# Sliding-window attention and a SwiGLU block: AV and scores in one block of 64x64 PE tiles per chunk

## Chip, cores, metric

One NeuronCore of a Trainium2 chip (trn2). The metric is the device time of one execution in microseconds (us).

A ratio of two kernels is the mean time of the one's fast runs over the mean time of the other's fast runs of the same rounds, on the same chip, with a 95% interval. It is not quite the ratio of the medians, which are quoted beside it.

## The reference, cut

Causal attention with a window of 64 keys, then a gated feed-forward block:

```python
# q, k, v: (8, 8, 576, 64) float32; w_gate, w_val: (512, 1536); w_out: (1536, 512)
scores = (q @ k.T) / 8                       # per batch and head
mask = (rel >= 0) & (rel < 64)               # rel = query position - key position
attn = softmax(where(mask, scores, -1e9))
x = (attn @ v), heads joined                 # (4608, 512)
g = x @ w_gate
out = ((g * sigmoid(g)) * (x @ w_val)) @ w_out
```

## The kernel before

The 4608 tokens are worked in 36 *chunks* of 128; four chunks are a *group* of 512 (groups 0 to 8). Every operation is recorded in a graph, which adds the semaphores; the order on an engine is the order in which operations are recorded. The engines are named as in the profile: PE is TensorE (matmuls), PEld its weight loads, ACT ScalarE, DVE VectorE, POOL GpSimd, SP SyncE. Matmuls write into eight PSUM banks, ps, of 128 x 512 float32, which the kernel hands out in rings. PE's array can be used whole or in smaller tiles; the size of the tiles is the *tiling mode*, and 64*128 in a line of the profile is a tile of 64 rows and 128 columns. The names used below:

- **S(n)**, scores of chunk n: PE matmuls, exp on ACT (two, one per half of the heads), two multiplications by a 0/1 mask on VectorE.
- **A(n)** or AV: probabilities times V on PE; then on VectorE a reciprocal and a division (L467 and L470 before the change) for each half. The division writes xb.
- **XD(n)**: DMA transpose of xb into xT, the input of the feed-forward. Groups 0 and 1 transpose on PE instead (**X(n)**).
- **F(c, f)**: for group c and feature block f, four matmuls into a G bank and four into a V bank; tanh (sig) on ACT; uu and hT on VectorE. Twelve per group.
- **O(c, u)**: twelve matmuls for 128 output rows, a copy on ACT, a store.

A query sees its own 64-key block and the one before. The kernel before forms, for each 64 queries, a matmul over 128 consecutive keys. For that it needs V twice: va, and vb, which is va shifted by 64 keys and made by DMA copies.

```python
    # S: per 64 queries (w) a window of 128 keys; one 64x128 PE tile per head
    for w in range(2):
        k0 = 128 * n + 64 * w
        for c in range(4):
            for h in range(2):
                ps = slice(64 * h, 64 * h + 64)
                r = e.matmul(sv[h][:, w, c], self.kT[ps, c, k0:k0 + 128],
                             qT[ps, c, 64 * w:64 * w + 64], ...)
    # AV: contraction over 128 keys; 64 queries of output per 128x64 PE tile
    for j in range(4):
        h = 2 * j + half
        for w, vv in ((0, vb), (1, va)):
            r = e.matmul(av[64*w:64*w+64, j, :], pt[:, h, 64*w:64*w+64], vv[:, h, 0:65],
                         start=True, stop=True)
    # [...] PSUM banks: F rotates over four, O has one of its own, the rest over three
    self.rot = {"f": ([0, 1, 2, 3], 0), "o": ([4], 0), "a": ([5, 6, 7], 0)}
    # [...] steady loop, groups 2 to 7; n = 4c+u+4
    self.F(c, 3 * u)
    self.A(n)
    self.TD(n + 3)             # DMA transposes of K and Q, three chunks ahead
    self.F(c, 3 * u + 1)
    self.S(n + 1)
    self.XD(n)
    self.copy_v(n + 3)
    self.O(c - 1, u)
    self.F(c, 3 * u + 2)
```

The softmax here doesn't subtract the row's maximum and nothing guards it: scores larger than these inputs give would overflow.

## Time and profile before

| | before |
|---|---|
| median of 3 runs | 350.76 us (350.25 to 352.24) |
| span of the profiled run | 349.7 us |
| PE busy | 94% |
| period of one chunk, groups 4 to 6 | 8.70 us |
| of it three F, one O, attention | 5.19, 2.60, 0.91 us |

The page's first part, busy time and share of the span; from the groups, AV on PE (columns: line, engine, operation, tiles, count, busy us, mean ns, idle before it):

```profile
PE 328.2 (94%) x2615; PEld 159.2 (46%) x2659; DVE 216.1 (62%) x461; ACT 140.9 (40%) x248; POOL 108.5 (31%) x141
...
L461 PE MATMUL ps<-va,pt 128*64 128x65 bf16 x288 | 15.6, 198 | 0.0
L461 PE MATMUL ps<-vb,pt 128*64 128x65 bf16 x288 | 15.6, 198 | 0.1
```

A busy share does not tell what one chunk pays. The timeline does (columns: start us, duration us, engine, line, operation; in brackets idle time before it and what ended it). PE, one chunk, the sixteen AV rows between 194.55 and 194.79 cut to the first:

```profile
193.59 1.03 PE L515 MATMUL ps<-xT,Wv 128*128 128x512 bf16 x3
194.55 0.22 PE L461 MATMUL ps<-vb,pt 128*64 128x65 bf16 x1
...
194.92 1.04 PE L515 MATMUL ps<-xT,Wg 128*128 128x512 bf16 x4
195.79 1.03 PE L515 MATMUL ps<-xT,Wv 128*128 128x512 bf16 x4
196.75 0.41 PE L432 MATMUL ps<-qT,kT 64*128 64x64 bf16 x16
197.09 2.76 PE L539 MATMUL ps<-Wo,hT 128*128 128x512 bf16 x11
```

Matmuls of 512 columns start 0.216 us apart, so four need 0.86 us, but their row lasts 1.03 us: a duration includes about 0.17 us of pipeline latency, and the cost of a row is read from start to start. Four V matmuls from 193.59 end streaming at 194.45; the next F starts at 194.92: AV costs 0.47 us. Scores cost 0.44 us (196.65 to 197.09). (One of the V matmuls is missing from the record.) No idle is left between these rows: PE is the bound.

VectorE in the same chunk:

```profile
195.75 0.17 DVE L467 RECIPROCAL rc<-ps 128x4 f32<-128x4 f32 x1
195.96 0.42 DVE L470 TENSOR_TENSOR xb<-ps,rc 128x256 bf16<-128x256 f32 x1
...
196.50 0.42 DVE L470 TENSOR_TENSOR xb<-ps,rc 128x256 bf16<-128x256 f32 x1
...
198.16 0.75 DVE L448 TENSOR_TENSOR pt<-pt,mask 128x512 bf16<-128x512 bf16 x2
```

The divisions follow AV at once and the masks come last, where there is time.

The last thing to see is a group boundary: the first F of a group needs xT of all four chunks. PE, start of group 4:

```profile
166.63 1.04 PE L515 MATMUL ps<-xT,Wg 128*128 128x512 bf16 x4 [0.30 <-DMA xT<-xb]
```

The transpose of the fourth chunk arrives 0.30 us late here, and 0.18 us late at group 3; at the later boundaries it is in time. (These idle times are the brackets of the timeline. They count from the recorded end of the matmul before, so each is short by the 0.17 us of latency; all boundary idle is given so.)

### The profile page before, as it was taken

The page shows a single profiled execution, that of the slowest core. Times are in us where ns is not written, and L with a number is a line of the kernel's source. Part 1 is how long each engine was busy: PE and PEld are TensorE (multiplying, and loading weights), DVE is VectorE, ACT ScalarE, POOL GpSimd, SP SyncE. Part 2 cuts the span into 40 slices and gives each one's busy share as a digit, 9 for nine tenths or more (in the row PEclk, how much of TensorE's full clock was granted, in tenths as well). Part 3 has the DMA queues.
Part 4 walks back from the last instruction along what each step waited for, and adds up shares of the span by engine and source line. Part 5 has one row for each costly group of instructions (what it writes and reads, how often), then busy time and mean ns, then how long its engine had stood idle before and what let it go on. Part 6 is the DMA issues. An engine that isn't in the chain of part 4 may idle for free.

```text
span 349.7 us, 6706 instructions
## 1 busy us (share of the span) xinstructions
PE 328.2 (94%) x2615; PEld 159.2 (46%) x2659; DVE 216.1 (62%) x461; ACT 140.9 (40%) x248; POOL 108.5 (31%) x141
## 2 busy tenths in 40 slices
PE   6686997899999999999999999999999999999996
PEld 2454443554444444444444444444444444444444
DVE  4655583478966666666666666666666666655520
ACT  3652444555543333444344444444433333232321
POOL 8996523364633343323232243222000000000000
PEclk9899899999999999999999999999999999999999
DMA  8999999999999999999999999999833311100012
GB/s 205 189 213 175 214 161 202 146 154 142 166 97 144 148 135 142 138 138 146 132 138 140 142 116 164 125 162 128 138 97 97 88 49 47 64 32 30 30 46 106
DMA packets 167279, 44.82 MB, mean 128 GB/s; under 512 B 147408, under 2 KB 162768, under 8 KB 167248
## 3 DMA queue, kind: packets, MB, share of 16 engines
q0 software_dynamic: 113152, 17.83, 71.7%
q1 hardware_dynamic: 51872, 25.38, 33.1%
q10 hardware_dynamic: 2224, 1.18, 1.3%
q8 instruction: 21, 0.34, 0.4%
q14 instruction: 10, 0.08, 0.1%
HBM read 37.75 MB, written 9.44 MB: 135 GB/s over the span
## 4 chain that ended last, share of the span: by engine, by line
PE 73%; DVE 10%; DMA 7%; POOL 5%; ACT 3%; issue 1%; POOLq 0%
PE ps L515 42%; PE ps L539 25%; DMA kn<-in_k_dram 4%; DVE uu L523 4%; DMA xT<-xb 3%; DVE hT L525 3%; PE ps L432 3%; PE ps L461 2%; ACT sig L521 2%; POOL Wg L365 2%; POOL Wv L365 1%; DVE xb L470 1%; PE ps L568 1%; POOL va L343 1%; PE ps L383 1%
## 5 line engine op out<-in xcount | busy, mean ns | idle before, releaser
L523 DVE SCALAR_TENSOR_TENSOR uu<-sig,ps 128x512 bf16<-128x512 bf16 (+1 forms) x112 | 74.4, 665 | 92.6 <-ACT sig L521 92.5
L515 PE MATMUL ps<-xT,Wg 128*128 128x512 bf16 (+1 forms) x435 | 110.2, 374 | 2.6 <-DVE uu L523 1.0
L515 PE MATMUL ps<-xT,Wv 128*128 128x512 bf16 (+1 forms) x433 | 111.3, 373 | 0.8
L521 ACT ACTIVATE sig<-ps 128x512 bf16<-128x512 f32 (+1 forms) x112 | 65.2, 582 | 95.0 <-PE ps L515 95.0
L539 PE MATMUL ps<-Wo,hT 128*128 128x512 bf16 x404 | 94.1, 379 | 3.8 <-DVE hT L525 1.7
L525 DVE SCALAR_TENSOR_TENSOR hT<-uu,ps 128x512 bf16<-128x512 bf16 (+1 forms) x112 | 74.8, 668 | 4.3 <-PE ps L515 0.5
L515 PEld LDWEIGHTS ps<-xT,Wv 128*128 128x128 bf16 x448 | 44.0, 98 | 50.1 <-issue 1.1
L343 POOL DMA_DIRECT2D va<-in_v_dram x40 | 34.1, 856 | 98.8 <-PE ps L461 97.5
L539 PEld LDWEIGHTS ps<-Wo,hT 128*128 128x128 bf16 x420 | 38.8, 98 | 46.1 <-DVE hT L525 1.6
L515 PEld LDWEIGHTS ps<-xT,Wg 128*128 128x128 bf16 x448 | 40.3, 98 | 42.8 <-DMA xT<-xb 1.5
L443 ACT ACTIVATE pt<-ps 128x512 bf16<-128x512 f32 x72 | 39.0, 596 | 21.5 <-PE ps L432 21.5
L551 ACT ACTIVATE ost<-ps 128x512 f32<-128x512 f32 x35 | 20.9, 597 | 62.3 <-PE ps L539 62.3
L267 POOL DMA_DIRECT2D qn<-in_q_dram x36 | 30.3, 844 | 38.6 <-PE ps L383 24.4
L470 DVE TENSOR_TENSOR xb<-ps,rc 128x256 bf16<-128x256 f32 x72 | 30.5, 424 | 2.5
L267 POOL DMA_DIRECT2D kn<-in_k_dram x36 | 30.5, 852 | 1.6 <-DMA qn<-in_q_dram 0.8
L448 DVE TENSOR_TENSOR pt<-pt,mask 128x512 bf16<-128x512 bf16 x64 | 24.4, 419 | 3.7 <-ACT pt L443 3.5
L461 PEld LDWEIGHTS ps<-vb,pt 128*64 128x64 bf16 x288 | 11.7, 110 | 13.4 <-DVE hT L525 9.7
L432 PEld LDWEIGHTS ps<-qT,kT 64*128 64x128 bf16 x576 | 10.4, 95 | 16.2 <-DVE rc L467 10.6
L432 PE MATMUL ps<-qT,kT 64*128 64x64 bf16 x576 | 14.5, 191 | 1.8 <-DVE xb L470 1.6
L461 PE MATMUL ps<-va,pt 128*64 128x65 bf16 x288 | 15.6, 198 | 0.0
L461 PE MATMUL ps<-vb,pt 128*64 128x65 bf16 x288 | 15.6, 198 | 0.1
L467 DVE RECIPROCAL rc<-ps 128x4 f32<-128x4 f32 x72 | 12.4, 172 | 0.9 <-PE ps L461 0.9
(52 smaller groups left out, 96.6 us busy)
## 6 DMA issues: line engine op xcount, KB each, us to landing
out_dram<-ost SPq DMA_DIRECT2D x35, 256.0 KB, 2.9
vb<-va SPq DMA_DIRECT2D x68, 80.0 KB, 4.1
va<-in_v_dram POOLq DMA_DIRECT2D x32, 128.0 KB, 4.7
qn<-in_q_dram POOLq DMA_DIRECT2D x28, 128.0 KB, 4.9
kn<-in_k_dram POOLq DMA_DIRECT2D x28, 128.0 KB, 5.3
Wo<-in_moe_w_out_dram POOLq DMA_DIRECT2D x2, 768.0 KB, 18.5
Wg<-in_moe_w_gate_dram POOLq DMA_DIRECT2D x5, 256.0 KB, 13.1
Wv<-in_moe_w_val_dram POOLq DMA_DIRECT2D x5, 256.0 KB, 13.6
```

What stands on the lines that cost most here:

```text
L267: self.g.op("pool", lambda e, d=d, a=a: e.dma_start(d, a), writes=ks, dma=True)
L343: g.op("pool", lambda e, d=d, a=a: e.dma_start(d, a), writes=ks, dma=True)
L432: r = e.matmul(sv[h][:, w, c], self.kT[ps, c, k0:k0 + 128], qT[ps, c, 64 * w:64 * w + 64], start=not biased, stop=not biased or (w == 1 an ...
L443: g.op("act", lambda e, po=po, si=si: e.activation(po, si, ACTF.Exp, scale=SCALE), reads=[bk], writes=[pk])
L448: g.op("dve", lambda e, po=po, m=m: e.tensor_tensor(po, po, m, ALU.mult), reads=[pk, "mask"], writes=[pk])
L461: r = e.matmul(av[64 * w:64 * w + 64, j, :], pt[:, h, 64 * w:64 * w + 64], vv[:, h, 0:65], start=True, stop=True)
L470: g.op("dve", lambda e: e.tensor_tensor(xo, av[:, :, 0:64], rb, ALU.mult), reads=[bk, ("rc", ir)], writes=[("xb", ix, half)])
L515: r = e.matmul(bank[:, 0:n], W[:, kk, f * 128:f * 128 + 128], xT[:, kk, t0:t1], start=(kk == 0), stop=(kk == NK - 1))
L521: g.op("act", lambda e: e.activation(sig[:, 0:n], G[:, 0:n], ACTF.Tanh, scale=0.5), reads=[gk], writes=[("sig", i)])
L523: g.op("dve", lambda e: e.scalar_tensor_tensor(uu[:, 0:n], sig[:, 0:n], 1.0, G[:, 0:n], ALU.add, ALU.mult), reads=[("sig", i), gk], writes ...
L525: g.op("dve", lambda e: e.scalar_tensor_tensor(hT[:, f, t0:t1], uu[:, 0:n], 0.5, V[:, 0:n], ALU.mult, ALU.mult), reads=[("uu", i), vk], wr ...
L539: r = e.matmul(OB[:, :], hT[:, f, 128 * u:128 * u + 128], self.Wo[:, f, :], start=(f == 0), stop=(f == NF - 1))
```

## The change

Intent: contract over aligned blocks of 64 keys, so that both scores and AV use 64x64 tiles, four at a time, in the same tiling mode. Then the scores of the next chunk can stand inside AV of this one, with fewer changes of tiling mode; V is needed once, without shifted copies; and one mask serves all chunks. AV of one head and 64 queries becomes two accumulating matmuls on two row tiles. To keep two row tiles from writing one PSUM bank at the same time (the rule is in the last section), AV has two phases, and the second waits for the end of the first; the scores fill this wait.

```diff
-        self.rot = {"f": ([0, 1, 2, 3], 0), "o": ([4], 0), "a": ([5, 6, 7], 0)}
+        self.rot = {"f": ([0, 1, 2, 3], 0), "a": ([4, 5, 6, 7], 0)}
 [...] S
-                for c in range(4):
+            for c in range(4):
+                for o, q0, q1, kk in ((0, 0, 128, k0), (64, 0, 64, k0 - 64), (64, 64, 128, k0 + 64)):
                     for h in range(2):
-                        r = e.matmul(sv[h][:, w, c], self.kT[ps, c, k0:k0 + 128],
-                                     qT[ps, c, 64 * w:64 * w + 64], ...)
+                        r = e.matmul(sv[h][o:o + 64, c, q0:q1], self.kT[ps, c, kk:kk + 64], qT[ps, c, q0:q1], ...)
 [...] A(n, mid): 16 matmuls of phase 0, then mid(), then 16 of phase 1
+        first = g.op("pe", phase(0), reads=rd, writes=wr)
+        if mid is not None:
+            mid()
+        g.op("pe", phase(1), reads=rd, writes=wr, after=[first])
         [...] then, for each half, reciprocal and division on VectorE
 [...] steady loop
                 self.F(c, 3 * u)
-                if live:
-                    self.A(n)
+                if live:
+                    self.A(n, (lambda: self.S(n + 1)) if n + 1 < NCH else None)
 [...]          self.TD(n + 3)
+                if live and c > 1:
+                    self.XD(n)
                 self.F(c, 3 * u + 1)
-                [...] self.S(n + 1); self.XD(n); self.copy_v(n + 3)
                 self.O(c - 1, u)            # its bank now comes from "a", no longer from "o"
                 self.F(c, 3 * u + 2)
```

`mid()` records all of S, its VectorE masks too, ahead of the divisions of A. Groups 0 and 1 and the start are rearranged in the same manner; there O takes banks of the F ring.

More of the change, by code (lines that the diff above doesn't have):

```diff
@@ L40, in __init__, with op @@
         self.readers = {}
-    def op(self, eng, fn, reads=(), writes=(), dma=False):
-        deps = {}
+    def op(self, eng, fn, reads=(), writes=(), dma=False, after=()):
+        deps = {o.i: (o, "sync") for o in after}
         for k in reads:
             for w in self.writers.get(k, ()):
-                deps[w.i] = (w, "raw")
+                deps.setdefault(w.i, (w, "raw"))
         for k in writes:
@@ L86, in emit @@
             for d, kind in deps:
-                if d.eng == e and not d.dma and (e == "pe" or kind != "raw") and not o.dma and e != "pool":
+                if kind != "sync" and d.eng == e and not d.dma and (e == "pe" or kind != "raw") and not o.dma and e != "pool":
                     continue
@@ L176, in alloc @@
         self.ident = sb("ident", 128)
-        self.mask = sb("mask", 4 * 64)
+        self.mask = sb("mask", 128)
         self.Wg = sb("Wg", NK * DFF)[:, :].rearrange("p (c f) -> p c f", c=NK)
@@ L184, in alloc @@
         self.va = [hd(t) for t in ring("va", self.NV, H * 80)]
-        self.vb = [hd(t) for t in ring("vb", self.NV, H * 80)]
         self.kT = sb("kT", 4 * (T + 64))[:, :].rearrange("p (c t) -> p c t", c=4)
@@ L191, in alloc @@
         self.cq, self.ck = [[t.rearrange("p (j h d) -> p j h d", j=2, h=H) for t in st(x, BF)] for x in ("cq", "ck")]
-        self.nmask = sb("nmask", 4 * 64)
+        self.nmask = sb("nmask", 128)
         self.wz = sb("wz", 512)
@@ L233, in init @@
         g.op("dve", lambda e: e.memset(self.kT[:, :, 0:64], 0.0), writes=[("kT", -1, p) for p in range(4)])
-        g.op("dve", lambda e: e.memset(self.vb[0][0:64, :, 0:66], 0.0), writes=[("vb", 0, 0)])
         self.init_va(0)
@@ L240, in init_va @@
             va = self.va[i]
-            g.op(eng, lambda e, va=va: e.memset(va[:, :, 64:80], 1.0), writes=[("va", i)])
+            g.op(eng, lambda e, va=va: e.memset(va[:, :, 64:80], 1.0), writes=[("va", i)],
+                 after=[self.last_sel] if eng == "pool" else [])
     def init_pool_a(self):
@@ L249, in init_mask @@
     def init_mask(self, m, key, fill):
-        mm = m[:, :].rearrange("p (a q) -> p a q", a=4)
-        self.g.op("pool", lambda e: e.affine_select(
-            out=mm, in_=mm, compare_op=ALU.is_gt, fill=fill, base=0,
-            pattern=[[0, 4], [-1, 64]], channel_multiplier=1), writes=[key])
-        self.g.op("pool", lambda e: e.affine_select(
-            out=mm, in_=mm, compare_op=ALU.is_ge, fill=fill, base=64,
-            pattern=[[0, 4], [1, 64]], channel_multiplier=-1), writes=[key])
-        self.g.op("pool", lambda e: e.memset(m[0:64, 128:192], fill), writes=[key])
+        for p0, c0, op in ((0, 0, ALU.is_ge), (0, 64, ALU.is_gt), (64, 0, ALU.is_gt), (64, 64, ALU.is_ge)):
+            d = m[p0:p0 + 64, c0:c0 + 64]
+            sg = 1 if op == ALU.is_gt else -1
+            self.last_sel = self.g.op("pool", lambda e, d=d, op=op, sg=sg: e.affine_select(
+                out=d, in_=d, compare_op=op, fill=fill, base=0,
+                pattern=[[-sg, 64]], channel_multiplier=sg), writes=[key])
     def load_qk(self, n):
@@ L284, in first_cast @@
             self.g.op("act", lambda e: e.activation(d, a, ACTF.Copy), reads=rk, writes=wk)
-    def first_vb(self, n, part, eng):
-        i = n + 1 - part
-        dst = self.vb[i][64:128] if part else self.vb[i][0:64]
-        src = self.va[n][0:64] if part else self.va[n][64:128]
-        rd, wr = [("va", n, 0), ("va", n, 1), ("va", n)], [("vb", i, part)]
-        if eng == "dve":
-            self.g.op("dve", lambda e: e.tensor_copy(dst, src), reads=rd, writes=wr)
-        else:
-            self.g.op("sp", lambda e: e.dma_start(dst, src), reads=rd, writes=wr, dma=True)
     def first_T(self, which, st):
@@ L332, in warm, with load_v @@
         self.g.op("pe", pe, reads=["wz"], writes=[bk])
-    def load_v(self, n, copy=True):
+    def load_v(self, n):
         g = self.g
@@ L343, in load_v @@
             g.op("pool", lambda e, d=d, a=a: e.dma_start(d, a), writes=ks, dma=True)
-        if copy:
-            self.copy_v(n)
-    def copy_v(self, n):
-        g = self.g
-        i = n % self.NV
-        va = self.va[i]
-        parts = list(self.segs(128 * n, 128))
-        vb = self.vb[i]
-        lo = [("va", i, 0), ("va", i)]
-        hi = [("va", i, 0 if len(parts) == 1 else 1), ("va", i)]
-        g.op("sp", lambda e: e.dma_start(vb[64:128], va[0:64]), reads=lo, writes=[("vb", i, 1)], dma=True)
-        if n + 1 < NCH:
-            i2 = (n + 1) % self.NV
-            vb2 = self.vb[i2]
-            g.op("sp", lambda e: e.dma_start(vb2[0:64], va[64:128]), reads=hi, writes=[("vb", i2, 0)], dma=True)
     def load_w(self, which, a, b):
@@ L401, in TD @@
              writes=[("qT", iz, p) for p in range(4)], dma=True)
-    def variant(self, n):
-        b0 = (2 * n) % BPB == 0
-        b1 = (2 * n + 1) % BPB == 0
-        return slice(2, 4) if b0 else (slice(1, 3) if b1 else slice(0, 2))
     def bias(self, n):
         bb = [self.bank("a") for _ in range(2)]
-        nm = self.nmask[:, :].rearrange("p (a q) -> p a q", a=4)[:, self.variant(n)].unsqueeze(2).to_broadcast([128, 2, 4, 64])
+        nm = self.nmask[:, :].unsqueeze(1).to_broadcast([128, 4, 128])
         for bank, bk in bb:
-            bv = bank[:, :].rearrange("p (w c q) -> p w c q", w=2, c=4)
+            bv = bank[:, :].rearrange("p (c q) -> p c q", c=4)
             self.g.op("pe", lambda e, bv=bv: e.matmul(bv, self.ident[:, :], nm, start=True, stop=False),
@@ L423, in S @@
             bb = [self.bank("a") for _ in range(2)]
-        sv = [b[:, :].rearrange("p (w c q) -> p w c q", w=2, c=4) for b, _ in bb]
+        sv = [b[:, :].rearrange("p (c q) -> p c q", c=4) for b, _ in bb]
+        k0 = 128 * n + 64
         def pe(e):
-            for w in range(2):
-                k0 = 128 * n + 64 * w
-                for c in range(4):
+            for c in range(4):
+                for o, q0, q1, kk in ((0, 0, 128, k0), (64, 0, 64, k0 - 64), (64, 64, 128, k0 + 64)):
                     for h in range(2):
                         ps = slice(64 * h, 64 * h + 64)
-                        r = e.matmul(sv[h][:, w, c], self.kT[ps, c, k0:k0 + 128],
-                                     qT[ps, c, 64 * w:64 * w + 64], start=not biased,
-                                     stop=not biased or (w == 1 and c == 3))
+                        r = e.matmul(sv[h][o:o + 64, c, q0:q1], self.kT[ps, c, kk:kk + 64], qT[ps, c, q0:q1],
+                                     start=not biased, stop=not biased or c == 3 and kk != k0 - 64)
             return r
@@ L439, in S @@
         for h, (bank, bk) in enumerate(bb):
-            po = pt.rearrange("p (c e) (w q) -> p e w c q", e=2, w=2)[:, h]
-            si = bank[:, :].rearrange("p (w c q) -> p w c q", w=2, c=4)
+            po = pt.rearrange("p (c e) q -> p e c q", e=2)[:, h]
+            si = bank[:, :].rearrange("p (c q) -> p c q", c=4)
             pk = ("pt", ip, h)
@@ L445, in S, with A @@
                 continue
-            m = self.mask[:, :].rearrange("p (a q) -> p a q", a=4)[:, self.variant(n)]
-            m = m.unsqueeze(2).to_broadcast([128, 2, 4, 64])
+            m = self.mask[:, :].unsqueeze(1).to_broadcast([128, 4, 128])
             g.op("dve", lambda e, po=po, m=m: e.tensor_tensor(po, po, m, ALU.mult), reads=[pk, "mask"], writes=[pk])
-    def AV(self, n, half):
+    def A(self, n, mid=None):
         g = self.g
-        iv, ip, ix = n % self.NV, n % self.NP, n % 4
-        va, vb, pt = self.va[iv], self.vb[iv], self.pt[ip]
-        bank, bk = self.bank("a")
-        av = bank[:, 0:260].rearrange("p (h x) -> p h x", h=4)
-        def pe(e):
-            for j in range(4):
-                h = 2 * j + half
-                for w, vv in ((0, vb), (1, va)):
-                    r = e.matmul(av[64 * w:64 * w + 64, j, :], pt[:, h, 64 * w:64 * w + 64], vv[:, h, 0:65], start=True, stop=True)
-            return r
-        g.op("pe", pe, reads=[("pt", ip, half), ("va", iv), ("va", iv, 0), ("va", iv, 1), ("vb", iv, 0), ("vb", iv, 1)], writes=[bk])
-        ir = (2 * n + half) % 4
-        rc = self.rc[ir]
-        g.op("dve", lambda e: e.reciprocal(rc[:, :].unsqueeze(2), av[:, :, 64:65]), reads=[bk], writes=[("rc", ir)])
-        xo = self.xb[ix][:, :].rearrange("p (c e d) -> p e c d", e=2, d=64)[:, half]
-        rb = rc[:, :].unsqueeze(2).to_broadcast([128, 4, 64])
-        g.op("dve", lambda e: e.tensor_tensor(xo, av[:, :, 0:64], rb, ALU.mult),
-             reads=[bk, ("rc", ir)], writes=[("xb", ix, half)])
@@ new lines, in A @@
+        ip, ix = n % self.NP, n % 4
+        va, vp, pt = self.va[n % self.NV], self.va[(n - 1) % self.NV], self.pt[ip]
+        bb = [self.bank("a") for _ in range(2)]
+        av = [b[:, 0:260].rearrange("p (h x) -> p h x", h=4) for b, _ in bb]
+        seq = {}
+        for step in range(2):
+            for j in range(4):
+                for half in range(2):
+                    kp = half ^ step
+                    for w in range(2):
+                        if kp == w or (2 * n + w) % BPB:
+                            seq.setdefault((half, w), []).append((step, j, kp))
@@ new lines, in phase, with pe @@
+        def phase(step):
+            def pe(e):
+                for j in range(4):
+                    for w in range(2):
+                        for half in range(2):
+                            q = seq[half, w]
+                            key = (step, j, half ^ step)
+                            if key not in q:
+                                continue
+                            kp, h = half ^ step, 4 * half + j
+                            vv = vp if kp > w else va
+                            ks = slice(64 * kp, 64 * kp + 64)
+                            ws = slice(64 * w, 64 * w + 64)
+                            r = e.matmul(av[half][ws, j, :], pt[ks, h, ws], vv[ks, h, 0:65],
+                                         start=key == q[0], stop=key == q[-1])
+                return r
+            return pe
@@ new lines, in A @@
+        vk = [("va", m % self.NV, j) for m in ((n - 1, n) if n else (n,)) for j in range(2)]
+        vk += [("va", m % self.NV) for m in ((n - 1, n) if n else (n,))]
+        rd = [("pt", ip, 0), ("pt", ip, 1)] + vk
+        wr = [bk for _, bk in bb]
+        first = g.op("pe", phase(0), reads=rd, writes=wr)
+        if mid is not None:
+            mid()
+        g.op("pe", phase(1), reads=rd, writes=wr, after=[first])
+        for half, (bank, bk) in enumerate(bb):
+            ir = (2 * n + half) % 4
+            rc = self.rc[ir]
+            g.op("dve", lambda e, rc=rc, a=av[half]: e.reciprocal(rc[:, :].unsqueeze(2), a[:, :, 64:65]), reads=[bk], writes=[("rc", ir)])
+            xo = self.xb[ix][:, 256 * half:256 * half + 256].rearrange("p (h d) -> p h d", h=4)
+            rb = rc[:, :].unsqueeze(2).to_broadcast([128, 4, 64])
+            g.op("dve", lambda e, xo=xo, rb=rb, a=av[half]: e.tensor_tensor(xo, a[:, :, 0:64], rb, ALU.mult),
+                 reads=[bk, ("rc", ir)], writes=[("xb", ix, half)])
@@ L526, in F, with O @@
              reads=[("uu", i), vk], writes=[("hT", ih, f)])
-    def O(self, c, u, mid=None):
+    def O(self, c, u, mid=None, kind="a"):
         g = self.g
@@ L533, in O @@
         ost = self.ost[io]
-        OB, ok = self.bank("o")
+        OB, ok = self.bank(kind)
         def part(f0, f1):
@@ L562, in O_last @@
         for w, eng in ((0, "act"), (1, "dve")):
-            OB, ok = self.bank("o")
+            OB, ok = self.bank("a")
             cs = slice(256 * w, 256 * w + 256)
@@ L579, in O_last, with load @@
             g.op(q, lambda e, d=d, cs=cs: e.dma_start(self.out[r0:r0 + 128, cs], d), reads=[("osth", w)], dma=True)
-    def A(self, n):
-        self.AV(n, 0)
-        self.AV(n, 1)
     def build(self):
         W = lambda a, b: (self.load_w("g", a, b), self.load_w("v", a, b))
-        def load(n, copy=True):
+        def load(n):
             if n < NCH:
                 self.load_qk(n)
-                self.load_v(n, copy)
+                self.load_v(n)
         self.first_loads()
         self.init()
-        self.load_v(0, False)
+        self.load_v(0)
         self.init_pool_a()
-        self.load_v(1, False)
+        self.load_v(1)
         self.init_mask(self.nmask, "nmask", -30000.0)
@@ L600, in build @@
         W(1, 2)
-        self.load_v(2, False)
-        self.load_v(3, False)
+        self.load_v(2)
+        self.load_v(3)
         for f in range(2, 12, 2):
@@ L619, in build @@
         self.S(1, b1)
-        self.first_vb(0, 1, "dve")
         self.first_cast("k", 1)
@@ L623, in build @@
         tk = self.first_T("k", 1)
-        self.first_vb(0, 0, "dve")
-        self.first_vb(1, 1, "dve")
-        for n, part in ((1, 0), (2, 1), (2, 0), (3, 1), (3, 0)):
-            self.first_vb(n, part, "sp")
         self.A(0)
@@ L637, in build @@
         self.banks("a", [5, 6, 7, 4])
-        b2, b3 = self.bias(2), self.bias(3)
+        b2 = self.bias(2)
         self.F(0, 0, 0, 256)
+        b3 = self.bias(3)
         self.S(2, b2)
+        self.S(3, b3)
         self.F(0, 1, 0, 256)
-        self.S(3, b3)
+        self.F(0, 2, 0, 256)
         self.A(2)
-        self.F(0, 2, 0, 256)
         self.A(3)
+        self.F(0, 3, 0, 256)
         self.X(2, "act")
-        self.F(0, 3, 0, 256)
         self.X(3, "act")
-        self.banks("a", [5, 6, 7])
         self.init_va(4, "pool")
@@ L665, in build @@
         self.F(0, 7)
-        self.A(4)
+        self.A(4, lambda: self.S(5))
         self.F(0, 8)
-        self.S(5)
         load(7)
@@ L671, in build @@
         self.X(4, "act")
-        self.A(5)
+        self.T(6)
         self.F(0, 10)
-        self.T(6)
+        self.A(5, lambda: self.S(6))
         self.F(0, 11)
         self.X(5, "act")
+        self.T(7)
         load(8)
-        self.S(6)
-        self.O(0, 0)
-        self.T(7)
+        self.O(0, 0, None, "f")
+        self.A(6, lambda: self.S(7))
         load(9)
-        self.A(6)
-        self.O(0, 1)
-        self.S(7)
-        def mid():
-            self.X(6, "act")
-            self.T(8)
-        self.O(0, 2, mid)
-        self.A(7)
-        self.S(8)
-        self.O(0, 3, lambda: self.X(7, "act"))
+        self.O(0, 1, None, "f")
+        self.X(6, "act")
+        self.T(8)
+        self.O(0, 2, None, "f")
+        self.A(7, lambda: self.S(8))
+        self.O(0, 3, lambda: self.X(7, "act"), "f")
         self.T(9)
         load(10)
-        load(11, False)
+        load(11)
         for c in range(1, NFC):
@@ L700, in build @@
                 live = n < NCH
-                load(n + 4, False)
-                last = u == 3
-                late = c == NFC - 1 and last
+                load(n + 4)
+                late = c == NFC - 1 and u == 3
                 self.F(c, 3 * u)
                 if live:
-                    self.A(n)
+                    self.A(n, (lambda: self.S(n + 1)) if n + 1 < NCH else None)
                 if n + 3 < NCH and n + 3 >= self.ND:
                     self.TD(n + 3)
+                if live and c > 1:
+                    self.XD(n)
                 self.F(c, 3 * u + 1)
-                if live:
-                    if n + 1 < NCH:
-                        self.S(n + 1)
-                    if c > 1:
-                        self.XD(n)
-                    elif last:
-                        self.X(n, "act")
-                    if n + 3 < NCH:
-                        self.copy_v(n + 3)
                 if c > 1 and not late:
                     self.O(c - 1, u)
+                if live and c == 1 and u == 3:
+                    self.X(n, "act")
                 self.F(c, 3 * u + 2)
-                if live and c == 1 and not last:
+                if live and c == 1 and u < 3:
                     self.X(n, "act")
@@ L727, in build @@
                     self.O(c - 1, u)
-        self.banks("o", [0, 1, 2, 3])
         for u in range(3):
```

## The prediction

> **What bounds the kernel now.** TensorE. The page gives PE 94% busy; the chain of waits is 73% PE. From 190 us on, the timeline repeats one period per 128-token chunk, 8.69 us, with no PE idle in it: three F (8 matmuls, 1.73 us each), one O (12, 2.60 us), and 0.91 us of attention. AV costs 0.47 us (stream end of F 194.45, next F 194.92), scores 0.44 us (196.65 to 197.09). Only about 0.25 us of each is streaming (AV pairs start every 31 ns, score pairs every 27 ns); the rest is about 0.10 us on entering and 0.10 us on leaving. The Trainium skill, "TensorEngine Tiling (Array Packing)", Key Properties, says a change of tiling mode drains the engine; the gaps agree.
>
> **What the change saves.** With four 64x64 tiles AV still runs 8 matmuls per tile, so I expect no shorter stream; scores likewise (512 columns per tile). One block instead of two saves two of four mode changes, 0.20 us; the wait of the second AV phase on the first, beside scores of 0.24 us and a matmul latency of 0.20 us, gives back about 0.06. Block: about 0.77 us, saving 0.14 us per chunk, some 4 us in all if nothing else moved. The 68 V copies (5.4 MB of 44.8) go. At the start PE waits 2.65 us for K of chunk 4 (31.5 to 34.2), queued behind weights and five V copies; I expect it 1 to 2 us earlier. Chunks 4 to 11 save about 1 us more.
>
> **What it adds on the critical path.** VectorE and the banks. A and scores take four banks, O the fifth of a ring of four, so O gets AV half 0's bank and must wait for its division. That division is now queued behind both score masks. From the end of the first F (t=0): scores start 0.23, both exps end 0.45+1.08 later (as at 65.63 to 67.16), masks free VectorE at 2.15, reciprocal 0.21, division 0.42, 0.06 to PE: O starts at 2.85 to 2.95. Before, O starts at 2.64. So the period becomes about 8.95 us: +0.26 us over 24 chunks (groups 2 to 7), +6 us, although the PE block is shorter; PE will sit idle about 0.4 us before each O.
>
> Second, the last division ends at 3.3 instead of 2.5, so the DMA transpose xT<-xb of a group's fourth chunk starts 0.9 us later, with only 3.9 us until the next group's first F. It took 4.8 us at groups 2 and 3 (stall 0.3 us then), 2.3 to 3.3 later. V buffers are now held one chunk longer, so the V, Q, K loads run together just before it. I expect stalls near 1 us at two to four boundaries: +2 to +3 us.
>
> **Sum.** 350.8 - 2.5 (start and groups 0, 1) + 6 + 2.5 = 357; I shade towards no change: 355.5 us, 8 in 10 between 348.5 and 361. Faster by over 2%: 0.04; within 2%: 0.63; slower by over 2%: 0.33.
>
> **What would show it.** Right: PE idle before O released by the division xb; period 8.9 to 9.0 us; block near 0.77 us; xT<-xb ending idle at group boundaries; K of chunk 4 landing before 33 us. Wrong: no idle before O and period near 8.5; or a block over 1 us, meaning that 64x64 matmuls issue slower than four per 30 ns.
>
> **What would make it wrong.** Slower issue of 56 small matmuls (slower); two-fold faster AV streams, V copies holding up DMA more than I think, or a larger gain at the start, where the cold clock after the wait costs 1.6 us (faster).

## The result

| | before | after |
|---|---|---|
| median | 351.19 us (4 runs, 350.25 to 352.24) | 361.10 us (4 runs, 360.19 to 361.61) |
| ratio | | 1.0278 (1.024 to 1.0317) |
| span of the profiled run | 349.7 us | 359.2 us |
| first F of group 1 | 69.24 us | 66.91 us |
| first F of group 2 | 96.25 us | 94.53 us |
| first F of group 4 | 166.63 us | 169.32 us |
| first F of group 6 | 236.21 us | 243.67 us |

The change is slower by 2.8%. The last four rows, read from the PE timelines, show where: until group 2 the kernel after is 1.7 us ahead, and it loses from there on. The page's first part after:

```profile
PE 331.8 (92%) x3459; PEld 158.4 (44%) x3459; DVE 218.3 (61%) x457; ACT 140.9 (39%) x248; POOL 108.9 (30%) x143
...
L442 PE MATMUL ps<-va,pt 64*64 64x65 bf16 x1088 | 22.7, 197 | 0.4
```

PE, one chunk, after:

```profile
197.00 1.03 PE L506 MATMUL ps<-xT,Wv 128*128 128x512 bf16 x4
197.96 0.32 PE L442 MATMUL ps<-va,pt 64*64 64x65 bf16 x16
198.10 0.42 PE L398 MATMUL ps<-qT,kT 64*64 64x128 bf16 x24
198.35 0.32 PE L442 MATMUL ps<-va,pt 64*64 64x65 bf16 x16
198.60 1.04 PE L506 MATMUL ps<-xT,Wg 128*128 128x512 bf16 x4
199.48 1.03 PE L506 MATMUL ps<-xT,Wv 128*128 128x512 bf16 x4
200.72 2.76 PE L530 MATMUL ps<-Wo,hT 128*128 128x512 bf16 x12 [0.22 <-DVE xb L461]
```

The block itself is a success. The F before it ends streaming at 197.86 and the F after it starts at 198.60: 0.74 us, against 0.91 us for the two parts before. But O starts at 200.72, while the F before it ends streaming at 199.48 + 0.86 = 200.34. PE loses 0.38 us there. (The bracket says 0.22 us; it is short by the latency.) VectorE says why:

```profile
199.20 0.91 DVE L412 TENSOR_TENSOR pt<-pt,mask 128x512 bf16<-128x512 bf16 x2
200.03 0.17 DVE L458 RECIPROCAL rc<-ps 128x4 f32<-128x4 f32 x1
200.24 0.42 DVE L461 TENSOR_TENSOR xb<-ps,rc 128x256 bf16<-128x256 f32 x1
...
200.79 0.42 DVE L461 TENSOR_TENSOR xb<-ps,rc 128x256 bf16<-128x256 f32 x1
```

The masks now come first. Half 0's division ends at 200.66, and O, whose bank is that of AV half 0, starts 0.06 us later. The last division ends at 201.21, 3.35 us after the first F; before, at 196.92, it was 2.47 us.

The list of waits after the change names the same wait (columns: who waited for whom, us in total, times, longest):

```profile
PE ps L530 <- DVE xb L461: 5.8, 23, 0.3
...
PE ps L506 <- DVE hT L516: 3.0, 2, 1.6
PE ps L506 <- DVE uu L514: 2.3, 2, 1.2
```

The other two rows are the group boundaries, four idle times of 1.59, 1.20, 1.43 and 1.13 us, 5.35 us in all against 0.48 us before. Group 5 begins so, PE, the DMA queue (SP) and POOL, which issues the loads of V, Q and K:

```profile
204.19 1.03 PE L506 MATMUL ps<-xT,Wv 128*128 128x512 bf16 x4
206.64 1.02 PE L506 MATMUL ps<-xT,Wg 128*128 128x512 bf16 x4 [1.43 <-DVE hT L516]
```

```profile
201.24 1.21 SPq L488 DMA_TRANSPOSE xT<-xb  x1
```

```profile
199.97 0.88 POOL L264 DMA_DIRECT2D qn<-in_q_dram  x1
200.84 0.90 POOL L264 DMA_DIRECT2D kn<-in_k_dram  x1
```

PE's wait is put down to VectorE's hT, which belongs to the previous F, whose banks this F does not use. The DMA transpose issued at 201.24 landed 5.3 us later, at 206.5; the F starts 0.1 us after that. So the transpose is the likely releaser, and an experiment below tests it. At this boundary the kernel before saw a landing of 2.6 us and no wait; there the Q load was issued after the transpose, and not 1.3 us before it. SP and POOL before, then the landing of this transpose after and before (from the view of tile xT):

```profile
196.95 1.19 SPq L497 DMA_TRANSPOSE xT<-xb  x1
197.57 0.88 POOL L267 DMA_DIRECT2D qn<-in_q_dram  x1 [1.30 <-DMA qT<-qn]
```

```profile
DMA to landing us min/median/max: 5.3/5.3/5.3
```

```profile
DMA to landing us min/median/max: 2.6/2.6/2.6
```

The span grew by 9.5 us: -1.7 us until group 2, +4.9 us of boundary idle (5.35 - 0.48), and a remainder of 6.3 us over 24 chunks, 0.26 us each. The timeline confirms the remainder: group 6, at whose end no boundary waits, takes 35.83 us (243.67 to 279.50), 8.96 us per chunk against 8.70. It is the wait before O, 0.42 us on average (5.8 us in 23 brackets, and 0.17 us more each), less the 0.17 us that the block saves.

### The profile page after: what moved, and what is told of

It reads as the page before. It is cut to its first block, busy times and chain, and to the rows that moved or that the text cites. A ratio compares the mean times of both kernels' runs of the same rounds, so it can differ in the third digit from the quotient of the medians.

```text
span 359.2 us, 8166 instructions
## 1 busy us (share of the span) xinstructions
PE 331.8 (92%) x3459; PEld 158.4 (44%) x3459; DVE 218.3 (61%) x457; ACT 140.9 (39%) x248; POOL 108.9 (30%) x143
## 4 chain that ended last, share of the span: by engine, by line
PE 62%; DVE 14%; ACT 10%; DMA 7%; POOL 3%; issue 3%; SPq 0%
PE ps L506 30%; PE ps L530 26%; ACT pt L408 8%; DMA kn<-in_k_dram 5%; DVE xb L461 4%; DVE pt L412 4%; DVE uu L514 3%; DMA fk<-in_k_dram 3%; PE ps L442 2%; PE ps L398 2%; DVE hT L516 2%; DVE rc L458 1%; ACT sig L512 1%; POOL qn L264 1%; PE ps L559 1%
## 5 line engine op out<-in xcount | busy, mean ns | idle before, releaser
L506 PE MATMUL ps<-xT,Wg 128*128 128x512 bf16 (+1 forms) x448 | 111.9, 372 | 6.3 <-DVE hT L516 3.0
L530 PE MATMUL ps<-Wo,hT 128*128 128x512 bf16 x420 | 96.3, 380 | 6.3 <-DVE xb L461 5.8
L412 DVE TENSOR_TENSOR pt<-pt,mask 128x512 bf16<-128x512 bf16 x64 | 26.8, 425 | 8.9 <-ACT pt L408 7.0
L442 PE MATMUL ps<-va,pt 64*64 64x65 bf16 x1088 | 22.7, 197 | 0.4
L442 PEld LDWEIGHTS ps<-va,pt 64*64 64x64 bf16 x1088 | 15.0, 106 | 14.8 <-issue 12.7
L398 PE MATMUL ps<-qT,kT 64*64 64x64 bf16 (+1 forms) x864 | 15.5, 201 | 0.6 <-ACT qT L360 0.5
L398 PEld LDWEIGHTS ps<-qT,kT 64*64 64x64 bf16 x864 | 12.3, 108 | 2.1 <-ACT qT L360 0.8
L482 ACT ACTIVATE xT<-ps 128x512 bf16<-128x512 bf16 x12 | 7.2, 596 | 8.6 <-PE ps L473 8.6
```

The lines of the kernel that those rows point to most:

```text
L398: r = e.matmul(sv[h][o:o + 64, c, q0:q1], self.kT[ps, c, kk:kk + 64], qT[ps, c, q0:q1], start=not biased, stop=not biased or c == 3 and kk ...
L412: g.op("dve", lambda e, po=po, m=m: e.tensor_tensor(po, po, m, ALU.mult), reads=[pk, "mask"], writes=[pk])
L442: r = e.matmul(av[half][ws, j, :], pt[ks, h, ws], vv[ks, h, 0:65], start=key == q[0], stop=key == q[-1])
L506: r = e.matmul(bank[:, 0:n], W[:, kk, f * 128:f * 128 + 128], xT[:, kk, t0:t1], start=(kk == 0), stop=(kk == NK - 1))
L530: r = e.matmul(OB[:, :], hT[:, f, 128 * u:128 * u + 128], self.Wo[:, f, :], start=(f == 0), stop=(f == NF - 1))
```

## The experiments

My theory after the result: the new tiles and the block are good, and all the loss comes from one late event, the divisions, through two consumers, the bank that O takes and the fourth chunk's transpose. The first rival is that the 64x64 block itself costs more than it saves. The second is that the boundary waits are what the profile says, VectorE's uu and hT. Each ratio is against the kernel before, in the same rounds on the same chip. Differences to the kernel after are between rounds: the median of the kernel before was 351.19 us in its round and 350.12, 350.71 and 351.65 us in those of the experiments, so a difference of about 1 us between medians of different rounds is not resolved; for small terms the traces decide.

| run | median us | ratio (95%) |
|---|---|---|
| after | 361.10 | 1.0278 (1.024 to 1.0317) |
| e1_o_f | 352.81 | 1.0084 (1.0047 to 1.0121) |
| e2_div_first | 347.03 | 0.9906 (0.9883 to 0.9929) |
| e3_nv7 | 358.62 | 1.0249 (1.0215 to 1.0282) |
| e4_x_act | 355.90 | 1.0176 (1.014 to 1.0212) |
| e5_split | 359.36 | 1.024 (1.0198 to 1.0282) |
| e7_div_nv7 | 346.35 | 0.9869 (0.983 to 0.9908) |
| e8_copies | 364.51 | 1.0401 (1.0362 to 1.044) |
| e9_div_x | 344.30 | 0.9817 (0.978 to 0.9853) |
| e10_of_x | 346.21 | 0.9854 (0.982 to 0.9888) |
| e6_div_nv7_x | 344.26 | 0.98 (0.976 to 0.9839) |

All ten gave a correct result. All edits are to the kernel after the change.

### O in another bank (e1_o_f)

```diff
-                    self.O(c - 1, u)
+                    self.O(c - 1, u, None, "f" if live else "a")
```

> O of groups 2 to 7 takes a bank of the F ring, so it no longer shares one with AV half 0; nothing else moves. Bank theory (O waits for the division because of the shared bank): PE idle before O ended by the division xb goes from 5.8 us in all to near 0, the chunk period from 8.9-9.0 to about 8.6 us, but the transpose xT<-xb starts as late as before against an earlier next group, so each boundary stall grows by about 0.3 us: total about 361 - 6 + 1.2 = 356 us. Rival (the 64x64 block itself is what got dearer): O starts no earlier and the time stays at 361.

Measured: 352.81 us. (The trace is of the slowest of its four runs, 354.84 us; the reason is given with e8.) PE at the same place, start of group 5:

```profile
197.58 1.03 PE L506 MATMUL ps<-xT,Wv 128*128 128x512 bf16 x4
198.44 2.75 PE L530 MATMUL ps<-Wo,hT 128*128 128x512 bf16 x12
...
201.90 1.03 PE L506 MATMUL ps<-xT,Wv 128*128 128x512 bf16 x4
204.77 1.02 PE L506 MATMUL ps<-xT,Wg 128*128 128x512 bf16 x4 [1.84 <-DVE hT L516]
```

O follows F without a gap, and the period is 8.52 us (groups 6 and 7, where no boundary waits: 34.08 us for four chunks). The boundary idle was 1.49, 1.79, 1.84 and 1.59 us, 6.7 us in all instead of 5.35: of what O gave back, a third of a microsecond per boundary, on average, was lost at the next wait, as expected. The gain was larger than I had written, 8.3 us instead of 5: I had counted the change of the period (0.26 us) and not the wait (0.38 us). The shared bank is shown to be one of the two causes, and the first rival falls: with the same block of 64x64 matmuls the period is 0.18 us shorter than before the change.

### Divisions ahead of the masks (e2_div_first)

```diff
 in S:
-            g.op("dve", ... mask multiplication ...)
+            def mask(...): g.op("dve", ...)
+            mask() if hold is None else hold.append(mask)
 in A:
+        hold = []
         if mid is not None:
-            mid()
+            mid(hold)
         [...] reciprocals and divisions
+        for mask in hold:
+            mask()
```

> The two score masks are issued on VectorE after the four division instructions instead of before them; banks, PE order and loads unchanged. Queue theory (the masks, waiting for both exps, hold up the divisions): the wait before O vanishes (period about 8.55 us) and the transpose xT<-xb starts 0.8 us earlier, so the boundary stalls fall from 5.3 us in all to about 2 to 4: total 361 - 9 = about 352 us. If instead only the bank matters and the order does not, the time stays near 361.

Measured: 347.03 us, 0.9% faster than the kernel before and 5 us below the expected 352. VectorE in it:

```profile
191.55 0.42 DVE L465 TENSOR_TENSOR xb<-ps,rc 128x256 bf16<-128x256 f32 x1
...
192.44 0.75 DVE L413 TENSOR_TENSOR pt<-pt,mask 128x512 bf16<-128x512 bf16 x2
```

Half 0's division ends at 191.97. On PE the four V matmuls of F start at 191.66 and O at 192.52, 0.86 us later, which is their streaming time: O still shares its bank with AV half 0 and does not wait, because the division ends before PE gets there. So the loss before O needed both the shared bank and the order; either edit alone removes it. The boundary idle fell to 0.66, 1.12, 0.73 and 0.93 us, 3.4 us in all. Groups 0 and 1 gained about 1 us each, which I had not expected; the experiment e10_of_x below names the reason. The rest of the miss is the error of e1 again: the period was put at about 8.55 us and the gain at 6 us, but from 8.96 us to the 8.52 us of this run 24 chunks gain about 10 us.

### A larger V ring (e3_nv7)

```diff
-    NV = 6
+    NV = 7
```

> V ring of 7 instead of 6: a V buffer, now read by two chunks, may be refilled at the same chunk as in the kernel before. If the boundary stalls come from the V, Q, K loads bunched just ahead of the transpose (landing 5.0 to 5.5 us against 2.6 to 4.9 before), landing falls to 3 to 5 us and the stalls from 5.3 us to 2 to 3: about 358.5 us. If they come from the late division alone, landing stays at 5.0 to 5.5 us and the time at 361. The wait before O stays in both.

Measured: 358.62 us, as expected. The boundary idle fell to 0.25, 0.48, 0.65 and 1.21 us, and the landing of the fourth transpose from 5.5, 5.1, 5.3 and 5.0 us to 4.1, 4.4, 4.5 and 5.1 us. POOL shows what moved:

```profile
162.32 0.88 POOL L264 DMA_DIRECT2D qn<-in_q_dram  x1 [1.14 <-DMA qT<-qn]
```

With 7 buffers the loads run a chunk further ahead, and the Q load has to wait for the transpose of an earlier Q; its bunch reaches the queues later: Q is issued 0.2 us before the transpose here, 1.4 us before it in the kernel after. At the start of group 6 the Q load did not have to wait (it was issued 1.4 us before the transpose), and there the idle stayed at 1.21 us. Without a V copy each V buffer is read by two chunks, so a ring of 6 had become in effect one shorter. This is a cause of about 2.5 us by the medians; the boundary idle of the traces says 2.75 us.

### The fourth chunk without the DMA transpose (e4_x_act)

```diff
-                if live and c > 1:
+                if live and c > 1 and u < 3:
                     self.XD(n)
-                if live and c == 1 and u == 3:
+                if live and u == 3:
                     self.X(n, "act")
```

> The fourth chunk of each group is transposed on PE and copied by ACT after O instead of by the DMA transpose. If the boundary idle is the wait for the DMA transpose (the profile names VectorE or issue there), it vanishes: -5.3 us, +0.24 us of PE for each of 6 groups: about 357 us. If it is VectorE's uu and hT of the previous F, as the profile names, nothing changes.

Measured: 355.90 us, 5.2 us less than after. Start of group 4:

```profile
161.72 2.76 PE L530 MATMUL ps<-Wo,hT 128*128 128x512 bf16 x12 [0.22 <-DVE xb L461]
164.32 0.39 PE L473 MATMUL ps<-ident,xb 128*128 128x128 bf16 x4
...
165.41 1.03 PE L506 MATMUL ps<-xT,Wv 128*128 128x512 bf16 x4
166.27 1.03 PE L506 MATMUL ps<-xT,Wg 128*128 128x512 bf16 x4
```

The boundary idle is gone at all groups, for 0.22 us of PE each, while VectorE's uu and hT are where they were. So the boundary wait was for the DMA transpose; the releaser that the profile printed was wrong, and the second rival falls.

### Two blocks instead of one (e5_split)

```diff
-                    self.A(n, (lambda: self.S(n + 1)) if n + 1 < NCH else None)
+                    self.A(n)
                 self.F(c, 3 * u + 1)
+                if live and n + 1 < NCH:
+                    self.S(n + 1)
```

> In groups 1 to 7 the scores leave the AV block and stand again between the second F and O, as in the kernel before; the 64x64 tiles, banks, V ring and loads stay as after the change. Mode-change theory: AV alone now waits openly for its first phase (about 0.72 us) and the scores cost 0.44 us again, 1.16 us against 0.75 us for the one block; the wait before O vanishes since the masks now come after the divisions: period about 8.9 us, divisions 0.8 us earlier, boundary stalls about 1 to 2 us in all: total about 358 us. Rival (the 64x64 tiles themselves shorten the streams): AV about 0.3, scores about 0.3, period about 8.4 to 8.6 and total below 350 us.

Measured: 359.36 us, a period of 9.00 us (group 6) and 1.8 us of boundary idle, near the expected 358, 8.9 and 1 to 2 us. PE:

```profile
214.85 1.03 PE L506 MATMUL ps<-xT,Wv 128*128 128x512 bf16 x4
215.80 0.72 PE L442 MATMUL ps<-va,pt 64*64 64x65 bf16 x32
216.45 1.04 PE L506 MATMUL ps<-xT,Wg 128*128 128x512 bf16 x4
```

AV alone costs 0.74 us (215.71 to 216.45). The period of 9.00 us less three F and one O (7.79 us) leaves 1.21 us for AV and scores together, of which 0.47 us for the scores, against 0.74 us for the block and 0.91 us before the change. The tiles by themselves lose: the second phase waits openly. Only the block wins 0.17 us: it costs no more than AV alone, so the scores inside it are free. That the filled wait and the two saved mode changes bring this is argued from the gaps; no run has one without the other. There is no wait before O here, since the masks come after the divisions again.

### Both causes of the boundary idle (e7_div_nv7)

Divisions first and a V ring of 7.

> Divisions before masks and a V ring of 7 together. If the boundary stalls have these two causes, which add up (2.0 us gone with the first, 2.7 us with the second, of 5.3), about 0.5 to 1 us is left: total 347.0 - 2.5 = about 344.5 us. If the transpose is slow for another reason (its own latency of about 5 us whatever the loads do), the stalls stay near 3.4 us and the time near 347.

Measured: 346.35 us, a miss of 1.9 us. The idle at the boundaries was 0.45, 0.94, none and 1.06 us: 2.5 us, where I had expected 0.5 to 1. The two causes do not add up. At the boundary without idle the Q load had waited (it was issued at 193.30 us, after the transpose at 192.84); at the one with 1.06 us it had not (226.40, before the transpose at 226.93). The other traces show the same order. In the eight whose fourth chunks go through the DMA transpose (before, after, e1, e2, e3, e5, e7, e8), 44 landings of a fourth chunk are recorded: 4.1 to 5.6 us in the 27 cases where a Q load was issued first, 2.6, 3.3 and 3.4 us in the three where it was issued after the transpose, and 2.3 us in the 14 with no load near. No edit moved the Q load alone, so this is a regularity, not a cause shown.

### The V copies back, unread (e8_copies)

The kernel after, with the 68 copies issued again at their old places into spare buffers.

> The kernel after the change, with all shifted V copies issued again at their old places, into buffers that nobody reads. If the copies held up the load of K of chunk 4, it lands about 1.4 us later (34.2 instead of 32.8 us) and group 1 starts 1 to 2 us later; if their traffic also slowed the transposes, boundary stalls grow from 5.3 us to about 6: total 361 + 2 = about 363 us. If the copies cost nothing, 361 us.

Measured: 364.51 us, 3.4 us over the kernel after; more than the 2 us expected. PE at the start of chunk 4, in the order before, after, with the copies:

```profile
34.20 0.40 PE L383 MATMUL ps<-ident,kn 128*128 128x128 bf16 x4 [2.65 <-DMA kn<-in_k_dram]
...
34.66 1.79 PE L515 MATMUL ps<-xT,Wg 128*128 128x512 bf16 x4
```

```profile
32.80 0.40 PE L354 MATMUL ps<-ident,kn 128*128 128x128 bf16 x4 [1.79 <-DMA kn<-in_k_dram]
...
33.26 1.03 PE L506 MATMUL ps<-xT,Wg 128*128 128x512 bf16 x4
```

```profile
34.27 0.55 PE L367 MATMUL ps<-ident,kn 128*128 128x128 bf16 x4 [3.62 <-DMA kn<-in_k_dram]
```

The copies delayed K by 1.5 us (32.80 to 34.27). Group 1 starts at 69.27 us, 2.4 us later, and the boundaries take another 1.0 us (1.72, 1.44, 1.69 and 1.53 us, 6.4 us in all).

Not all of this is the copies. After the wait for K, PE ran some matmuls at half speed: four took 1.79 us in the kernel before and 1.91 us with the copies, instead of 1.03 us. The granted clock from 35 to 40 us was 0.68 and 0.72 in these two traces and 1.00 in that of the kernel after. But such a stretch comes and goes between executions of one kernel: the four runs of e1 had a mean clock of 0.99, 1.0, 1.0 and 1.0, and the first took 2.2 us longer than the mean of the others. In the trace of e1, whose start is that of the kernel after, K arrives just as early (32.77 us, after a wait of 2.19 us), the clock was 0.84 and 0.82 from 30 to 35 and 35 to 40 us, and group 1 started at 69.42 us. In e6 a wait of 2.59 us was followed by full clock. So the wait alone does not decide it, and of the 2.4 us only the 1.5 us of K are shown to be the copies'. Executions at the same mean clock of 0.995 are fairer: three with the copies took 363.93 to 364.62 us, two of the kernel after 361.27 and 361.61 us. Dropping the copies is a real gain of the change, of about 3 us.

### Divisions first, fourth chunk through PE (e9_div_x)

> Divisions before masks, and the fourth chunk of each group transposed on PE with its copy on ACT. If all the boundary idle is the wait for the DMA transpose, the 3.4 us left with the divisions first go and 6 times 0.24 us of PE come: total about 347.0 - 2.0 = 345 us. If the two edits share the same gain, it stays at 347.

Measured: 344.30 us, 1.8% faster than the kernel before (1.5 to 2.2%). No boundary waits; 0.7 us better than expected.

### The divisions left late, both consumers moved (e10_of_x)

The edits of e1 and e4 together.

> The divisions stay late (behind the masks, as after the change); only their two consumers are moved away: O takes an F bank, and the fourth chunk goes through PE and ACT. If the late division costs time only through these two, the period is 8.52 us without boundary stalls and the total equals that of divisions first with the PE transpose: about 344 to 346 us. If the lateness has a third consumer (F banks, VectorE's own queue), it stays above 348 us.

Measured: 346.21 us, just outside the expected range. From the first F of group 2 to that of group 8 both take 205.8 us (94.31 to 300.12 here, 92.43 to 298.25 in e9). But group 1 starts 1.0 us later than in e9 (66.80 against 65.81) and takes 0.9 us longer (27.51 against 26.62). The waits of e10, then of e9, name a third consumer, the PE transposes, most of them in groups 0 and 1:

```profile
PE ps L473 <- DVE xb L461: 4.0, 6, 0.8
```

```profile
PE ps L479 <- DVE xb L465: 1.8, 3, 0.7
```

2.2 us of difference, close to the 1.9 us in time. This is also what e2 gained in groups 0 and 1.

### All three (e6_div_nv7_x)

> Divisions first, V ring of 7, fourth chunk through PE and ACT. The V ring acted only through the landing of the boundary transpose, which is no longer waited for: no gain over the same kernel with a ring of 6, about 344 us. If the V ring frees something else (loads at the start, scores waiting for Q or K), it is faster, 342 to 343 us.

Measured: 344.26 us, a ratio of 0.98: the same as e9. The V ring mattered only to the boundary transpose. Each of groups 2 to 7 takes 34.3 us, which is four periods of 8.52 us and 0.22 us for the transpose on PE. PE has no wait left there. This version and e9 are the fastest; e2, e7 and e10 also beat both kernels, by less.

## Why the prediction was wrong

It had the direction, the mechanism and the stages right and the size wrong: 355.5 us (348.5 to 361) against 361.1 us, 0.1 us above the range. The step that failed is the landing of the fourth chunk's transpose at the group boundaries: the stalls that follow from it were put at half their size. Term by term:

- **Block of 0.77 us, saving 0.14 us per chunk.** Right: 0.74 us, saving 0.17 us. The Trainium skill ("TensorEngine Tiling (Array Packing)", Key Properties) says that a change of tiling mode drains the engine; the traces show about 0.10 us at each side of a block, and inside it, where AV and scores both use 64x64 tiles, only about 0.02 us between them (AV's last matmul starts near 198.08, 197.96 + 0.32 less 0.20 for one matmul, and the scores start at 198.10). e5 shows that without the common block the tiles lose.
- **O waits for half 0's division, behind both masks; +0.26 us per chunk, +6 us.** Right, and for the reason given: O starts 2.86 us after the first F (2.85 to 2.95 predicted), the idle before it is 0.38 us in the chunk shown, the division's end to O's start is 0.06 us, and the 24 chunks lost 6.3 us beside the boundaries. e1 and e2 removed it.
- **Start and groups 0 and 1, -2.5 us.** Too hopeful: -1.7 us. K of chunk 4 came 1.4 us earlier, as predicted, and the start gained 2.3 us in these two traces. Part of that is luck: the trace before has half-speed stretches and the trace after none (see e8), and in e1, whose trace has them too, group 1 started no earlier (69.42 us) than before the change (69.24 us). How much of the gain belongs to the change is not shown. And group 1 lost 0.6 us, where "save about 1 us more" had been written for chunks 4 to 11: the PE transposes wait for the late divisions, the third consumer of e10, which I had left out.
- **Boundary stalls, "near 1 us at two to four boundaries: +2 to +3 us".** This is the step that failed most: four boundaries, 1.13 to 1.59 us, +4.9 us. The slack I gave (3.9 us) was right, and the delay of the transpose (0.9 us) too. The landing was not: I took 4.8 us for some boundaries and 2.3 to 3.3 us for others from the trace before, though the same text said that the loads would now run together just before the transpose. They did so at every boundary that still had loads: Q was issued 1.3 to 1.4 us before the transpose, where at groups 5 and 6 before the change it had been issued 0.6 and 0.1 us after it. The landing was 5.0 to 5.5 us at all four. The case that I named should have been applied to all of them. Earlier divisions (e2) took 1.9 us off the boundary idle, a V ring of 7 (e3) 2.75 us, both together (e7) 2.9 us, and a fourth chunk without the DMA transpose (e4) all of it.
- **"I shade towards no change".** The sum was 357 us, and 1.5 us were taken off for no measured reason. The terms as measured are -1.7, +6.3 and +4.9 us, 9.5 us in all; since the 6.3 us are the remainder, this sum checks nothing by itself.

Among the things that were to make it wrong, slower issue of the small matmuls did not occur.

What stays open: the landing goes with the order of the Q load and the transpose (e7), but no run moved only that, and why it is 4.1 us in one group and 5.6 us in another with the Q load first in both is not settled.

## What to carry to other kernels

When two pieces of work are merged on the busy engine, look at the engine that serves both: its instructions are merged too, in recording order, and work with a near deadline (here the divisions) may end up behind work with a far one (the masks, needed a chunk later). Count the banks a merged block holds at once; the next user of the ring waits for whatever drains its bank. And when a wait is shortened, the time may be lost again at the next wait downstream, as e1 showed, so list all consumers of the late result before putting a number on it.

## What the Trainium skill lacked or had wrong

- "TensorEngine Tiling (Array Packing)", Key Properties: that a change of tiling mode drains the engine agrees with the traces, but no duration is given. Here it was about 0.10 us on entering and 0.10 us on leaving a block between 128*128 matmuls, 0.4 us of the 0.91 us of attention per chunk.
- The same page, Theoretical Speedup: "Up to 2×" is for a dimension of 64 or less; the page does not take up a contraction of 128 that is cut into two of 64 to get smaller tiles. Here that doubled the matmuls (576 to 1088 for AV) over twice as many tiles and did not shorten the stream: 0.12 us from the first start to the last in each AV phase (0.32 us less 0.20 for one matmul), 0.24 us together, as before (194.55 to 194.79). The gain came from the block alone.
- "PSUM — Partial Sum Buffer", PSUM bank collisions raise a hardware error: different row tiles must not access one bank at the same time, and software has to synchronize. The change obeys this and no run failed. The page gives no cost; AV with its two phases and nothing between them took 0.74 us against 0.47 us before, and scores between the phases hid it.
- "DMA: Bandwidth & Descriptors", Queues, rings and completion order: each DMA engine takes turns between its queues. Whether these turns delay the transposes here no run shows, and I found no page that gives the landing time of a small DMA transpose beside loads. One 128x512 bf16 transpose landed 2.3 us after issue with no loads left and, in the kernel after, 5.0 to 5.5 us with the V, Q and K loads queued just before it.
- No page that I read warns that the releaser printed for a PE wait can be an engine instruction long done when the real one is a DMA (the help of the profile view itself does): 1.13 to 1.59 us per boundary were put down to VectorE's uu or hT, and e4 showed the transpose.
